# Second layer of the last four experts by column halves, first outputs by column halves, left tokens' transfer by batches

## The chip, the cores and the metric

The kernel runs on one core of a Trainium2 chip. The metric is the device time of one execution in microseconds; the time before is 535.15 us, the median of three runs (534.55 to 535.35). Engines are named as in the profile: PE is TensorE, PEld its weight load, DVE VectorE, ACT ScalarE, POOL GpSimd, SP SyncE, which issues the transfers of this kernel.

## The reference

Attention of 8 batches with 8 heads, 576 positions of 64, in which scores under the row's maximum minus tau are dropped, and on its output x (4608 tokens of 512) a soft mixture of 8 experts with 4 slots each, hidden size 1024:

```python
attn_out = _attn_ref(q, k, v, tau)                       # 8, 8, 576, 64
x = attn_out.transpose(0, 2, 1, 3).reshape(4608, 512)
logits = x @ phi                                         # 4608 x 32
d = softmax(logits, axis=0)                              # 1e-09 added to the sum
slot_input = (d.T @ x).reshape(8, 4, 512)
for e in range(8):
    h = np.maximum(slot_input[e] @ w1[e], 0.0)           # 4 x 1024
    slot_out[e] = h @ w2[e]                              # 4 x 512
c = softmax(logits, axis=1)
return c @ slot_out.reshape(32, 512)                     # 4608 x 512
```

## The kernel before

The first 470 us hold the attention and, with it, the logits and the sums of slot_input; TensorE works there nearly without a stop. The change touches nothing of it, apart from four small copies of st1 to st4 at its end. Behind it comes the tail, which is written in the order in which each engine is to run it (`manual_schedule`).

The tail works on two groups of four experts (a = 0 for experts 0 to 3, a = 1 for 4 to 7). A group's four experts stand side by side on the 128 columns of TensorE, 32 each. Both layers' weights come in units of 1 MB: four units (one for each expert, index g) for each group and half K of the contraction. A unit of w2 is a tile of 128 partitions with four rows (j) of 512 floats each; `load_unit` issues a unit's transfer on SP once the tile's former user has left it. The last four units (`LAST`: a = 1, K = 1) come in parts: j 0 and 1 of all four, 512 KB each, then j 2 and 3 of the first three; j 2 and 3 of the fourth had been loaded long before into `early`.

`stage1` is the first layer, `relu` and `hidden` bring its result onto the partitions as hz, and `stage2` the second layer. It accumulates into the PSUM tile `so`, 512 columns, over both groups, all K and j; the partitions of so hold four partial sums. The last part (a = 1, K = 1, j 2 and 3) goes into two tiles `end` (h00e and h11e), one for each half of the 512 columns, so that `so` can be copied to SBUF (`so_sb`) meanwhile. `combine` then adds end to so_sb on DVE, sums the four parts by a matmul with st4 (tile sr) and splits the result in a high and a low part `sh` for the output product (ACT writes the cast, DVE the rest).

The output product takes the 128 partitions of cT, the transposed weights c of one batch, against sh. A batch's 512 tokens are four matmuls of 128 tokens, token 4p + c for partition p, so that one partition writes four rows of out that follow each other, 8 KB. Each 128x512 result is in a tile of its own (`otile`), copied to SBUF by ACT or DVE in turn. The batches' first 512 tokens go out in transfers of 1 MB, the first two batches in smaller pieces (256, 256 and 512 KB; 512 and 512 KB). Job 8 is the left tokens, 64 of each of the eight batches. `ct()` makes the next cT: POOL a block of c two ahead, four transposes on TensorE, cast on ACT, subtraction on DVE; it stands behind the batch's output matmuls, two batches ahead, with three cT buffers.

For the left tokens 128 partitions write 8 KB each, four tokens of one batch: partition = r * 8 + b, with r from 0 to 15.

Of the kernel before, what the change touches and what calls it, by code (L numbers as in the profile page):

```python
# [838 lines left out]
def softmax_attention_soft_moe(  # L839
# [104 lines left out]
    early = wp.tile([128, 2, 512], F32, name="early")  # L944

# [4 lines left out]
    def load_unit(t):  # L950
# [554 lines left out]
    st4 = tl.tile([128, 4, 32], F32, name="st4")  # L1505
    for g in range(4):
        nc.gpsimd.tensor_copy(st4[:, g, :], st1)
# [32 lines left out]
    def ct():  # L1540
# [9 lines left out]
        t = tl.tile([128, SM], F32R, tag="cT", name=f"cT{len(cTs)}", bufs=3)  # L1550
# [54 lines left out]
    def stage2(a, K, h):  # L1605
        w = range(n_units // 2 + (a * 2 + K) * 4, n_units // 2 + (a * 2 + K) * 4 + 4)
        t = [where[i].rearrange("p (j f) -> p j f", j=4) for i in w]

        if a == NG - 1 and K == 1 and h == 1:
            for n, g in enumerate((3, 0, 1, 2)):  # L1610
                for q, dst in enumerate(end):
                    x = slice(q * DM // 2, (q + 1) * DM // 2)
                    for j in (2, 3):
                        m = (n + q) % 2 * 2 + j - 2
                        nc.tensor.matmul(
                            dst[m * 32:(m + 1) * 32, 0:DM // 2], hz[a][:, K * 4 + j, g * 32:(g + 1) * 32],
                            t[g][:, j, x] if g < 3 else early[:, j - 2, x], start=n < 2, stop=n > 1,
                            tile_position=(0, 32 * m), skip_group_check=True)
            return
        for j in (2 * h, 2 * h + 1):  # L1620
            for g in range(4):
                nc.tensor.matmul(
                    so[g * 32:(g + 1) * 32, :], hz[a][:, K * 4 + j, g * 32:(g + 1) * 32], t[g][:, j],
                    start=(a, K, j) == (0, 0, 0), stop=(a, K, j) == (NG - 1, 1, 1),
                    tile_position=(0, 32 * g), skip_group_check=True)
# [18 lines left out]
    def combine():  # L1644
# [13 lines left out]
        for n, (b, k, z) in enumerate(jobs):  # L1658
# [17 lines left out]
            if k + z == 4:  # L1676
                ct()
# [81 lines left out]
```

## Time and profile before

| | us |
|---|---|
| median of 3 runs | 535.15 |
| lowest, highest | 534.55, 535.35 |
| profiled execution, first to last instruction | 533.2 |
| difference of the median to it | 1.95 |

The page gives busy shares over the whole span: PE 97%, DVE 88%, ACT 84%, POOL 46%. They belong to the attention. For the tail one takes the windows (busy time of each engine in a stretch, the granted clock as a share of the full one, the mean busy share of the 16 DMA engines and what they moved) and the chain of waits, which goes from the last instruction back to what released it. Times are counted from the first instruction. In the names of tiles, numbers of buffers are left out: "w" is any tile of weights, "host" any of those that the outputs are gathered in.

### The profile page before, as it was taken

How to read it: one execution, taken by the hardware profiler on the slowest of the kernel's cores; microseconds unless marked ns; L12 is line 12 of the kernel's file. 1: busy time of each engine (PE TensorE's matmuls, PEld its weight loads, DVE VectorE, ACT ScalarE, POOL GpSimd, SP SyncE). 2: the span in 40 equal slices, each digit the busy share in tenths (PEclk: the TensorE clock that was granted, in tenths of full speed). 3: DMA queues.
4: the chain of work that ended last, by engine and by line, in shares of the span. 5: the costliest groups of instructions: out<-in, count | busy, mean ns of one | idle time of the engine just before them, and what ended most of it. 6: DMA issues, size and time to landing. Idle time of an engine off the chain costs nothing.

```text
span 533.2 us, 21792 instructions
## 1 busy us (share of the span) xinstructions
PE 514.7 (97%) x8877; PEld 403.5 (76%) x8877; DVE 467.3 (88%) x1311; ACT 447.4 (84%) x750; POOL 247.6 (46%) x444
## 2 busy tenths in 40 slices
PE   8999999999999999999999999999999999999881
PEld 5877888888878888888788888888788877643470
DVE  6999998999899998999899989999999999613282
ACT  3899998999899989998999989999899899612271
POOL 2475554556446454655356635554464546021030
PEclk9999999999999999999999999999999999999996
DMA  6333335333337314732953355353466315999398
GB/s 157 94 93 94 93 98 172 96 94 93 94 99 245 93 35 100 256 78 67 284 140 96 92 172 173 94 133 94 104 225 188 83 20 176 368 401 389 158 399 301
DMA packets 28868, 83.26 MB, mean 156 GB/s; under 512 B 4064, under 2 KB 12256, under 8 KB 26336
## 3 DMA queue, kind: packets, MB, share of 16 engines
q1 hardware_dynamic: 28448, 81.43, 49.5%
q8 instruction: 70, 1.15, 0.9%
q10 hardware_dynamic: 320, 0.44, 0.3%
q14 instruction: 30, 0.25, 0.2%
HBM read 72.42 MB, written 9.44 MB: 154 GB/s over the span
## 4 chain that ended last, share of the span: by engine, by line
PE 86%; DMA 4%; ACT 3%; DVE 3%; issue 2%; SPq 0%; DVEq 0%; ACTq 0%
PE ps L1068 24%; PE ps L1211 22%; PE ps L984 19%; PE ps L1234 4%; PE ps L1223 4%; PE ps L1073 3%; DMA w<-in_w 3%; PE ps L1268 2%; PE h L1579 2%; PE ps L1326 2%; PE ps L1376 2%; PE ps L1178 1%; ACT cT L1570 1%; DVE cT L1571 1%; PE ct L976 1%
## 5 line engine op out<-in xcount | busy, mean ns | idle before, releaser
L1080 DVE TENSOR_SCALAR_CACHE_REDUCE ss<-ps 128x576 f32<-128x576 f32 x288 | 208.3, 751 | 4.6 <-PE ps L1068 1.4
L1096 DVE SCALAR_TENSOR_TENSOR p<-ss,thr,p 128x576 f32<-128x576 f32 x256 | 203.6, 821 | 3.8 <-POOL thr L1093 1.6
L1093 POOL TENSOR_SCALAR thr<-nmx,pabs 128x1 f32<-128x1 f32 x288 | 136.1, 480 | 146.5 <-DVE ss L1080 143.2
L1090 ACT ACTIVATE p<-ss,nmx 128x576 f32<-128x576 f32 x256 | 188.6, 781 | 12.6 <-DVE ss L1080 11.6
L1068 PE MATMUL ps<-k,q 64*128 64x288 f32 x1024 | 154.9, 423 | 0.4
L1068 PEld LDWEIGHTS ps<-k,q 64*128 64x128 f32 x1024 | 87.5, 188 | 23.6 <-ACT pTa L989 5.1
L984 PEld LDWEIGHTS ps<-ident,p 64*128 64x128 f32 x2304 | 91.8, 138 | 17.2 <-DVE ss L1080 2.3
L984 PE MATMUL ps<-ident,p 64*128 64x64 f32 x2304 | 101.4, 223 | 0.2
L989 ACT COPY pTb<-ps 128x1024 f32<-128x1024 f32 (+1 forms) x96 | 83.8, 877 | 2.1 <-PE ps L984 0.7
L989 ACT COPY pTa<-ps 128x1024 f32<-128x1024 f32 x64 | 65.1, 1017 | 0.4 <-PE ps L984 0.2
L1211 PE MATMUL ps<-pTa,vv 128*64 128x128 f32 x992 | 61.0, 276 | 0.1
L1211 PE MATMUL ps<-pTb,vv 128*64 128x128 f32 x992 | 60.4, 274 | 0.0
L1211 PEld LDWEIGHTS ps<-pTa,vv 128*64 128x64 f32 x992 | 53.5, 137 | 5.5 <-issue 4.3
L1211 PEld LDWEIGHTS ps<-pTb,vv 128*64 128x64 f32 x992 | 53.6, 137 | 3.3 <-issue 2.8
L1263 POOL TENSOR_TENSOR x<-x,ri 128x512 f32<-128x512 f32 x31 | 37.2, 1201 | 10.3 <-ACT x L989 10.3
L1122 POOL TENSOR_SCALAR pL<-pL,ri 128x576 f32<-128x576 f32 x31 | 26.0, 840 | 15.2 <-DVE ri L1121 14.2
L1048 POOL TENSOR_SCALAR k<-k,flag 128x576 f32<-128x576 f32 x31 | 31.7, 1023 | 0.8 <-DMA k<-in_kT 0.4
L989 ACT COPY pTl<-ps 128x256 f32<-128x256 f32 x64 | 27.5, 429 | 3.3 <-PE ps L984 2.9
L1119 POOL TENSOR_SCALAR ri<-r 128x9 f32<-128x9 f32 x31 | 7.1, 229 | 45.4 <-DVE p L1096 44.6
L1223 PE MATMUL ps<-pTl,vv 64*64 64x128 f32 x496 | 26.5, 284 | 0.5 <-DVE ss L1080 0.5
L1249 ACT COPY xT<-ps 128x256 f32<-128x256 f32 x62 | 23.2, 374 | 4.4 <-PE ps L1211 2.6
L1532 POOL TENSOR_TENSOR w<-lall,crow 128x512 f32<-128x512 f32 x9 | 9.3, 1046 | 37.7 <-PE ct L976 24.4
(175 smaller groups left out, 609.0 us busy)
## 6 DMA issues: line engine op xcount, KB each, us to landing
w<-in_w SPq DMA_DIRECT2D x18, 1024.0 KB, 8.2
q<-in_qT SPq DMA_DIRECT2D x62, 288.0 KB, 4.5
vv<-in_vt SPq DMA_DIRECT2D x32, 320.0 KB, 4.8
host<-in_w SPq DMA_DIRECT2D x10, 1024.0 KB, 8.2
k<-in_kT SPq DMA_DIRECT2D x62, 144.0 KB, 4.2
out<-host SPq DMA_DIRECT2D x7, 1024.0 KB, 6.9
w<-in_w SPq DMA_DIRECT2D x7, 512.0 KB, 14.4
out<-host SPq DMA_DIRECT2D x2, 512.0 KB, 3.0
```

Of the source, the lines that this page charges most:

```text
L984: nc.tensor.transpose(out=s[:, g, c:c + 64], in_=ins[g], identity=ident[rows[g], rows[g]], tile_position=(64 * g, 0))
L989: G.add("ACT", 51 + 0.833 * n, nom, lambda: nc.scalar.copy(*io()), r, w)
L1048: sc = lambda e, kc=kc: lambda: e.tensor_scalar(out=kt.t[:, kc], in0=kt.t[:, kc], scalar1=flag8, **one)
L1068: nc.tensor.matmul(s.t[:, g, 0:HS], qt.t[rows[g], h, c * 128:(c + 1) * 128], kt.t[rows[g], h * HS:(h + 1) * HS], start=True, stop=True, ti ...
L1080: dve(678, t + OFF['mx'], [s], [ss, nmx], lambda s=s, ss=ss, nmx=nmx: nc.vector.tensor_scalar(out=ss.t.rearrange("p (a k) -> p a k", a=2), ...
L1090: G.add("ACT", 674, t + OFF['ex'], lambda sv=sv, nmx=nmx, view=view: nc.scalar.activation(view().rearrange("p (a k) -> p a k", a=2), sv(), ...
L1093: pool(250, t + OFF['th'], pre=75, fn=lambda nmx=nmx, thr=thr: nc.gpsimd.tensor_scalar(out=thr.t, in0=nmx.t, scalar1=1.0, scalar2=pabs, op ...
L1096: fn=lambda sv=sv, thr=thr, view=view, i=i: nc.vector.scalar_tensor_tensor(out=view().rearrange("p (a k) -> p a k", a=2), in0=sv(), scalar ...
L1122: pool(725, t + OFF['sc'], lambda: nc.gpsimd.tensor_scalar(out=pL.t[:, SL:SL + S], in0=pL.t[:, SL:SL + S], scalar1=ri.t[:, 8:9], **one), [ ...
L1211: nc.tensor.matmul(area(w, h, l)[rows[a]], vv.t[:, (h * 4 + kb) * 64:][:, 0:64], pT.t[:, h, kb, a * 128:(a + 1) * 128], tile_position=(0, ...
L1223: nc.tensor.matmul(area(ab[l], h, l)[rows[a]], vv.t[rows[h], SM + h * 64:][:, 0:64], pTl.t[rows[h], (l * 2 + a) * 128:][:, 0:128], tile_po ...
L1263: G.add("POOL", 1040, u + 6.8, own=f"new{j}" + group(b), r=[ri], w=[x[j]], fn=lambda: nc.gpsimd.tensor_tensor(out=wide(), in0=wide(), in1= ...
```

## The change

- The last four units of w2 come by column halves: 256 of 512 columns, all four j (512 KB in rows of 1 KB) of the first three, j 0 and 1 (256 KB) of the fourth; then the same for the other half. Eight transfers in place of seven, the same bytes.
- `so` takes the first group alone and is copied behind it. The second group goes by column halves into the two end tiles: `half(q, j)` the units of K = 0, `half_unit(q, g)` one unit of K = 1. Column half 0 is complete before half 1 begins.
- `total(q)` is combine's first part for one half; total(0) stands in the middle of half(1, .), total(1) behind the first outputs.
- `out_half(b, q)` puts out one column half of batch b, 0 to 3: two tiles of 128x2x256 with two matmuls of 256 columns each, one copied by ACT, one by DVE, and a transfer of 512 KB in rows of 1 KB. Half 0 of the four batches stands between the half_units of column half 1; half 1 behind total(1), each with a ct. Batches 4 to 7 and the left tokens go whole, by `out_whole`.
- The left tokens' transfer has b outermost, partition = b * 16 + r; cT8 is written in that order.
- st4 lies in a tile of w2 that is free there and is copied behind stage 1; otile uses so's bank in place of h11's; cT has four buffers.

The diff, cut to its core:

```diff
-        for k, h in [(i, 0)] * (i in LAST) + [(k, 1) for k in LAST[:-1]] * (i == LAST[-1]):
-            nc.sync.dma_start(where[k].rearrange("p (j f) -> p j f", j=4)[:, 2 * h:2 * h + 2],
-                              src(units[k][1])[:, 2 * h:2 * h + 2])
+        for k, q in [(i, 0)] * (i in LAST) + [(k, 1) for k in LAST] * (i == LAST[-1]):
+            js = slice(0, 2 if k == LAST[-1] else 4)
+            nc.sync.dma_start(where[k].rearrange("p (j f) -> p j f", j=4)[:, js, cols[q]], src(units[k][1])[:, js, cols[q]])
...
-        t = tl.tile([128, SM], F32R, tag="cT", name=f"cT{len(cTs)}", bufs=3)
+        t = tl.tile([128, SM], F32R, tag="cT", name=f"cT{len(cTs)}", bufs=4)
...
-            tv = t.rearrange("p (c r b) -> p b r c", c=4, b=B)
+            tv = t.rearrange("p (c b r) -> p b r c", c=4, b=B)
...
+    def product(a, K, j, g, m, w, dst, q, **kw):
+        nc.tensor.matmul(dst[m * 32:(m + 1) * 32, 0:q.stop - q.start], hz[a][:, K * 4 + j, g * 32:(g + 1) * 32], w[:, q],
+                         tile_position=(0, 32 * m), skip_group_check=True, **kw)
...
+    def half(q, j):
+        t = w2_units(NG - 1, 0)
+        for g in range(4):
+            product(NG - 1, 0, j, g, g, t[g][:, j], end[q], cols[q], start=j == 0, stop=False)
+
+    def half_unit(q, g):
+        t = w2_units(NG - 1, 1)[g]
+        for j in (2, 3, 0, 1):
+            w = early[:, j - 2] if g == 3 and j > 1 else t[:, j]
+            product(NG - 1, 1, j, g, j, w, end[q], cols[q], start=False, stop=g == 3)
+
+    def total(q):
+        x = cols[q]
+        nc.vector.tensor_tensor(out=so_sb[:, x], in0=end[q][:, 0:DM // 2], in1=so_sb[:, x], op=ALU.add)
+        w = ttile(f"sr{q}")
+        nc.tensor.matmul(w[:, 0:DM // 2], st4.rearrange("p g s -> p (g s)"), so_sb[:, x], start=True, stop=True)
+        nc.scalar.copy(sh[:, x], w[:, 0:DM // 2])
+        nc.vector.scalar_tensor_tensor(
+            out=sh[:, x], in0=sh[:, x].bitcast(F32), scalar=neg, in1=w[:, 0:DM // 2], op0=ALU.mult, op1=ALU.add)
...
+    def out_half(b, q):
+        ot = through()[b].rearrange("p (c d) -> p c d", c=4)[:, :, cols[q]]
+        for k in range(2):
+            w = otile(f"o{b}_{q}_{k}").rearrange("p (c d) -> p c d", c=2)
+            for c in range(2):
+                nc.tensor.matmul(w[:, c], cTs[b][:, token(b, 2 * k + c)], sh[:, cols[q]], start=True, stop=True,
+                                 skip_group_check=True)
+            if k:
+                nc.vector.tensor_copy(ot[:, 2 * k:2 * k + 2], w)
             else:
-                nc.sync.dma_start(out.rearrange("(b s) d -> b s d", s=S)[:, SM:S].rearrange(
-                    "b (r c) d -> r b (c d)", c=4), ot.rearrange("p c d -> p (c d)"))
+                nc.scalar.copy(ot[:, 2 * k:2 * k + 2], w)
+        nc.sync.dma_start(out[b * S:b * S + SM].rearrange("(p c) d -> p c d", c=4)[:, :, cols[q]], ot)
...
+            nc.sync.dma_start(out.rearrange("(b s) d -> b s d", s=S)[:, SM:S].rearrange(
+                "b (r c) d -> b r (c d)", c=4), ot.rearrange("p c d -> p (c d)"))
...
+    for K in range(2):
+        stage2(0, K)
+        if K == 0:
+            hidden(1)
+    nc.scalar.copy(so_sb, so)
+    for j in range(4):
+        half(0, j)
+    for g in range(4):
+        half_unit(0, g)
+    for j in range(4):
+        half(1, j)
+        if j == 1:
+            total(0)
+    for g in range(4):
+        half_unit(1, g)
+        out_half(g, 0)
+        if g < 2:
+            ct()
+    total(1)
+    for b in range(4):
+        out_half(b, 1)
+        ct()
+    for b in range(4, B + 1):
+        out_whole(b)
```

How TensorE's order moves. Before, from the last four units' second half to the second output job (h00e and h11e are the end tiles, early and w11, w5, w1 the units' tiles, w7 the hidden values, sr the sums with st4, o the outputs as job and chunk, ct a transposed block of c):

```order
L1615 MATMUL h11e_8448<-w5_114,w7_116 32x256 x2
L1615 MATMUL h00e_8447<-w1_110,w7_116 32x256 x2
L1615 MATMUL h11e_8448<-w1_110,w7_116 32x256 x2
L1651 MATMUL sr0_8548<-w3_112,st4_8278 128x256
L1651 MATMUL sr1_8552<-w3_112,st4_8278 128x256
L1664 MATMUL o0_0_0_8556<-sh_8302,cT0_8416 128x256
L1664 MATMUL o0_0_1_8559<-sh_8302,cT0_8416 128x256
L1671 MATMUL o1_0_8563<-sh_8302,cT0_8416 128x512
L1671 MATMUL o2_0_8567<-sh_8302,cT0_8416 128x512
L1671 MATMUL o2_1_8568<-sh_8302,cT0_8416 128x512
L976 MATMUL ct2_8575<-ident_61,w3_112 128x128 x4
L1671 MATMUL o3_0_8583<-sh_8302,cT1_8432 128x512
```

After, from the first unit of column half 1 to the third batch's first half:

```order
L1608 MATMUL h11e_8448<-w11_120,w7_116 32x256 x4
L1663 MATMUL o0_0_0_8563<-sh_8297,cT0_8416 128x256 x2
L1663 MATMUL o0_0_1_8567<-sh_8297,cT0_8416 128x256 x2
L977 MATMUL ct2_8574<-ident_61,w3_112 128x128 x4
L1608 MATMUL h11e_8448<-w5_114,w7_116 32x256 x4
L1663 MATMUL o1_0_0_8585<-sh_8297,cT1_8432 128x256 x2
L1663 MATMUL o1_0_1_8589<-sh_8297,cT1_8432 128x256 x2
L977 MATMUL ct3_8596<-ident_61,w3_112 128x128 x4
L1608 MATMUL h11e_8448<-w1_110,w7_116 32x256 x4
L1663 MATMUL o2_0_0_8607<-sh_8297,cT2_8573 128x256 x2
```

Before, all of the second layer lies ahead of sr and of every output. After, half_unit (h11e), four o matmuls of one batch and a ct follow each other in turn, and sr1 stands behind the fourth batch's first half:

```order
L1608 MATMUL h11e_8448<-w8_117,w7_116 32x256 x2
L1663 MATMUL o3_0_0_8620<-sh_8297,cT3_8595 128x256 x2
L1663 MATMUL o3_0_1_8624<-sh_8297,cT3_8595 128x256 x2
L1635 MATMUL sr1_8630<-w3_112 128x256
L1663 MATMUL o0_1_0_8634<-sh_8297,cT0_8416 128x256 x2
L1663 MATMUL o0_1_1_8638<-sh_8297,cT0_8416 128x256 x2
L977 MATMUL ct4_8645<-ident_61,w3_112 128x128 x4
L1663 MATMUL o1_1_0_8652<-sh_8297,cT1_8432 128x256 x2
```

From there on a batch's second half and one ct take turns.

SP's queue before, the last parts of w2 (w11 to w1) and the outputs (out; the numbers are partitions by floats):

```order
L965 DMA w11_120<-in_w2 128x1024
L965 DMA w5_114<-in_w2 128x1024
L965 DMA w1_110<-in_w2 128x1024
L1679 DMA out_0<-w10_119 128x512 x2
L1679 DMA out_0<-w10_119 128x1024
L1679 DMA out_0<-host0_7724 128x1024 x2
L1679 DMA out_0<-host1_7882 128x2048
L1679 DMA out_0<-host2_7980 128x2048
L1679 DMA out_0<-host3_8054 128x2048
L1679 DMA out_0<-host4_8062 128x2048
```

And after, from the second column half:

```order
L967 DMA w11_120<-in_w2 128x4x256
L967 DMA w5_114<-in_w2 128x4x256
L967 DMA w1_110<-in_w2 128x4x256
L967 DMA w8_117<-in_w2 128x2x256
L1669 DMA out_0<-w10_119 512x1x256
L1669 DMA out_0<-host0_7724 512x1x256
L1669 DMA out_0<-host1_7882 512x1x256
L1669 DMA out_0<-host2_7980 512x1x256
L1669 DMA out_0<-w10_119 512x1x256
L1669 DMA out_0<-host0_7724 512x1x256
```

Two whole transfers and five pieces of batches 0 to 3 have become eight halves of 512 rows of 256 floats, and the weights come as 128x4x256; the last transfer, at the end of the same queue, is 8x16x2048 for 16x8x2048.

## Rows read from the trace of the kernel before

**Rows 1.** Page, chain that ended last: share of the span by engine.

```profile
PE 86%; DMA 4%; ACT 3%; DVE 3%; issue 2%; SPq 0%; DVEq 0%; ACTq 0%
```

**Rows 2.** Chain of waits 490 to 534: start us, us, what.

```profile
481.25 15.94 DMA w<-in_w
...
501.70 0.43 DVE w L1648
...
502.18 0.71 PE sr L1651 x2
502.91 0.38 ACT sh L1652
...
503.32 0.49 DVE sh L1653
...
503.94 0.85 PE o L1664 x2
...
506.78 0.70 DVE cT L1571
...
507.62 0.64 PE ct L976 x4
```

**Rows 3.** Windows: span, length, busy of engines, granted clock, DMA share, GB/s.

```profile
40.00:100.00 60.00, 59.92 (x1144) 49.75 (x1140) 58.01 (x166) 57.09 (x98) 31.70 (x56) 1.00 0.42 111
491.40:497.20 5.80, 5.67 (x46) 1.41 (x38) 0.00 (x0) 0.00 (x0) 0.00 (x0) 1.00 1.01 408
502.00:506.00 4.00, 3.19 (x14) 2.62 (x15) 2.15 (x6) 1.94 (x5) 0.00 (x0) 1.00 0.00 0
505.00:517.00 12.00, 10.36 (x49) 8.68 (x49) 10.57 (x17) 9.01 (x18) 5.24 (x5) 1.00 0.89 356
517.00:527.00 10.00, 4.05 (x16) 2.79 (x15) 5.89 (x9) 4.49 (x8) 0.00 (x0) 0.90 1.02 416
524.00:526.00 2.00, 0.00 (x0) 0.00 (x0) 0.00 (x0) 0.00 (x0) 0.00 (x0) 0.73 1.04 434
527.00:528.00 1.00, 0.00 (x0) 0.00 (x0) 0.00 (x0) 0.00 (x0) 0.00 (x0) 0.50 1.02 262
528.00:529.00 1.00, 0.00 (x0) 0.00 (x0) 0.00 (x0) 0.00 (x0) 0.00 (x0) 0.50 1.02 197
531.00:532.00 1.00, 0.00 (x0) 0.00 (x0) 0.00 (x0) 0.00 (x0) 0.00 (x0) 0.50 0.04 16
527.00:532.00 5.00, 0.00 (x0) 0.00 (x0) 0.00 (x0) 0.00 (x0) 0.00 (x0) 0.50 0.74 208
```

**Rows 4.** Timeline of TensorE 495 to 506: start us, us, line, tile.

```profile
500.97 0.41 PE L1615 MATMUL h00e<-w,w 128*32 128x256 f32 x2 [0.53 <-DMA w<-in_w]
```

**Rows 5.** Timeline of SyncE, 66 to 90 and 495 to 534.

```profile
67.37 1.34 SPq L1425 DMA_DIRECT2D phi_sb<-in_phi  x1
69.39 0.35 SPq L1053 DMA_DIRECT2D vv<-in_vt  x1
...
505.32 1.42 SPq L1679 DMA_DIRECT2D out<-w  x3
```

**Rows 6.** DMA view 505 to 515: 40 bins of 0.25 us.

```profile
GB/s 0 0 0 0 90 385 385 377 377 401 459 393 426 393 410 99 279 442 410 377 426 393 410 393 410 393 262 524 426 328 295 524 524 426 262 328 524 426 393 360
```

**Rows 7.** Groups by form 494 to 534: line engine op names shapes, busy, mean ns.

```profile
L1671 PE MATMUL o<-sh,cT 128*128 128x512 f32 x35 | 12.3, 472 | 1.2 <-DVE cT L1571 1.2
L1675 DVE COPY host<-o 128x512 f32<-128x512 f32 x16 | 10.2, 686 | 0.2
L1671 PEld LDWEIGHTS o<-sh,cT 128*128 128x128 f32 x35 | 9.2, 301 | 2.0 <-DVE cT L1571 1.5 <-DVE host L1675 0.2
...
L1622 PE MATMUL so<-w,w 128*32 128x512 f32 x32 | 5.4, 595 | 0.2 <-DMA w<-in_w 0.2
...
L976 PEld LDWEIGHTS ct<-ident,w 128*128 128x128 f32 x28 | 3.0, 140 | 3.7 <-POOL w L1532 3.0 <-issue 0.6
L1615 PE MATMUL h00e<-w,w 128*32 128x256 f32 x12 | 2.2, 387 | 0.5 <-DMA w<-in_w 0.5
```

More of the change, by code (lines that the diff above doesn't have):

```diff
@@ L944, in softmax_attention_soft_moe @@
     early = wp.tile([128, 2, 512], F32, name="early")
+    cols = [slice(n * DM // 2, (n + 1) * DM // 2) for n in range(2)]
     def load_early():
@@ L1603, in hidden, with w2_units @@
                 )
-    def stage2(a, K, h):
+    def w2_units(a, K):
         w = range(n_units // 2 + (a * 2 + K) * 4, n_units // 2 + (a * 2 + K) * 4 + 4)
[L1607 to L1620, printed above, removed]
-            for g in range(4):
[L1622 to L1625, printed above, removed]
-        if h:
-            for i in w:
-                load_unit(where[i])
@@ new lines, in w2_units, with stage2 @@
+        return [where[i].rearrange("p (j f) -> p j f", j=4) for i in w]
+    def product(a, K, j, g, m, w, dst, q, **kw):
+        nc.tensor.matmul(dst[m * 32:(m + 1) * 32, 0:q.stop - q.start], hz[a][:, K * 4 + j, g * 32:(g + 1) * 32], w[:, q],
+                         tile_position=(0, 32 * m), skip_group_check=True, **kw)
+    def stage2(a, K):
+        t = w2_units(a, K)
+        for j in range(4):
+            for g in range(4):
+                product(a, K, j, g, g, t[g][:, j], so, slice(0, DM), start=(K, j) == (0, 0), stop=(K, j) == (1, 3))
@@ L1634, in otile @@
         k = cnt[0] % 6
-        return ps_h.tile([128, 512], F32, tag=("h01", "h10", "h11")[k // 2], name=name) if k % 2 else ttile(name)
+        return ps_h.tile([128, 512], F32, tag=("h01", "h10", "so")[k // 2], name=name) if k % 2 else ttile(name)
     def through():
@@ new lines, in out_whole @@
+    def out_whole(b):
+        ot = through()[b].rearrange("p (c d) -> p c d", c=4)
+        ws = [otile(f"o{b}_{c}") for c in range(4)]
+        for c in range(4):
+            nc.tensor.matmul(ws[c], cTs[b][:, token(b, c)], sh, start=True, stop=True)
+            if c % 2 == 0:
+                nc.scalar.copy(ot[:, c], ws[c])
+            else:
+                nc.vector.tensor_copy(ot[:, c], ws[c])
+        ct()
+        if b < B:
+            nc.sync.dma_start(out[b * S:b * S + SM].rearrange("(p c) d -> p c d", c=4), ot)
+        else:
+            nc.sync.dma_start(out.rearrange("(b s) d -> b s d", s=S)[:, SM:S].rearrange(
+                "b (r c) d -> b r (c d)", c=4), ot.rearrange("p c d -> p (c d)"))
@@ L1698, in softmax_attention_soft_moe @@
         relu(a, hp[a])
+    st4 = where[2][:, 3 * DM:3 * DM + 128].rearrange("p (g s) -> p g s", g=4)
+    for g in range(4):
+        nc.gpsimd.tensor_copy(st4[:, g, :], st1)
     ct()
@@ L1701, in softmax_attention_soft_moe @@
     end[:] = [ps_h.tile([128, 512], F32, tag=t, name=t + "e") for t in ("h00", "h11")]
-    for a in range(NG):
-        for K in range(2):
-            for h in range(2):
-                if a == NG - 1 and K == 1 and h == 1:
-                    nc.scalar.copy(so_sb, so)
-                stage2(a, K, h)
-            if a < NG - 1 and K == 0:
-                hidden(a + 1)
-    combine()
+    for K in range(2):
[7 more added lines that the diff above has]
+        half_unit(0, g)
+    for j in range(4):
+        half(1, j)
+        if j == 1:
+            total(0)
+    for g in range(4):
+        half_unit(1, g)
[5 more added lines that the diff above has]
+        out_half(b, 1)
+        ct()
+    for b in range(4, B + 1):
+        out_whole(b)
     order_all.close()
```

39 lines of the change are left out of this document (2 added, 37 removed).

## The prediction

> **What bounds the kernel now.** I read first the chain of waits of the last 44 us, then the windows of the same stretch, then single groups. Over the whole span the chain is 86% TensorE [rows 1], but the change touches nothing ahead of about 480 us, so only the tail counts. There the chain [rows 2] is to be read as four pieces. Until 497 us it is the transfer of the second layer's weights: DMA w<-in_w ends at 497.19, and the windows give 408 GB/s at a share of 1.01, so the sixteen DMA engines are full [rows 3]. From the last weights (TensorE takes the last of them at 500.97, after a wait for DMA [rows 4]) to the first output transfer runs a serial chain: add, sr, ACT sh, DVE sh, o, tile copies, first issue at 505.32 [rows 2, 5]. In it the DMA engines stand still: 502 to 506 moves nothing [rows 3]. From 506 the outputs go out. Within 505:517 356 GB/s, which is 4.27 MB: the first four batches (4 x 1.05 = 4.19 MB) are out at 516.9. Behind it, until 527, DMA is the bound (416 GB/s). Then a last piece is slow: the last transfer, of the left tokens. From 527 on 208 GB/s x 5.0 us = 1.04 MB go, which is just its 1 MB, and it ends at about 531.1; at the 434 GB/s of 524:526 the same would take 2.4 us, and it takes 4.1 [rows 3]. So two things are to be had: the 4 to 6 us in which DMA stands, and 1.7 us of the last transfer.
>
> **The change, part by part.** The profiled execution has 533.2 us between its first and last instruction, the median of the runs is 535.15; I add terms to the median and take the 1.95 us between the two as constant.
>
> *Loads by column halves.* The first half now is 1.835 MB (w8 has its other half in `early`) where 2.10 MB stood ahead of 497.19: 0.26 MB less at 408 GB/s is -0.64 us. But rows get short, 1 KB in place of 4 KB. In the transfers by row size [rows 6] four bins of 2 KB rows go at 381 GB/s on average and the next four, of longer rows, at 420: about 10% for that step, so I take 10% for 1 KB rows: 1.835 MB / 408 = 4.5 us, +0.45. First half in at 497.0, second at about 501.3 (before 500.9). Bounds: 0% to 60% (a rival, below).
>
> *The first chain.* From 497.0: four matmuls of 256 columns, half of the 0.86 us that four of 512 take (387 and 595 ns each, overlapped by two [rows 7]), then add 0.43, sr 0.71, ACT 0.38, DVE 0.49 [rows 2]. The two groups of half(1,.) that stand between the last unit and sr run during the add and cost some 0.3 beyond it. Before, this chain took 4.35 us from 500.97 to 505.32; now one add and one sr less (-0.8), half(1,.) +0.3, and a tile copy that waits for four o matmuls, not for one (+1.2): 5.1 us, so the first issue falls at 502.1, 3.2 us earlier.
>
> *The middle.* Here TensorE's order decides, since each out_half stands behind the next half_unit and ahead of a ct. A batch costs four o matmuls, whose strided weights load for 301 ns against 140 for ct [rows 7] and which follow each other at about 0.235 us, 0.94; a ct, 0.44 without its drain; a half_unit 0.43; two changes of tile shape, some 0.1 each: 2.0 us. The 512 KB that it gives go out in 1.4. Issues at 502.1, 504.1, 506.1 and, without ct, 507.4. So DMA idles again by 0.5 us three times.
>
> *The second chain.* total(1) stands behind out_half(3,0) and is serial: 0.43 + 0.71 + 0.38 + 0.49 and hand-overs, 2.3 us, and 1.95 until the first tile of the second half is out: 507.4 to 511.6. DMA idles for 2.8 us. The single serial chain has become two. Then a second half costs VectorE a tile copy of 0.69 and the subtraction of a cT of 0.70 [rows 2, 7], 1.45 us a batch, about what its transfer takes. Issues 511.6, 513.2, 514.7, 516.1; batch 4, with two tile copies on VectorE behind ct7, at 518.2, its data from 519.0. Before, it was 516.9: +2.1. A replay of the engines' queues with the same durations gives +1.3 for it; I keep 2.1. Issuing costs SP more: phi's 512 pieces took it 1.34 us where 128 took 0.35 [rows 5], about +1.0 for each of the fourteen 512-piece transfers. SP has waits of over that everywhere but in the second halves (1.34 of 1.45); +0.2 for the last of these. Bounds of the whole of this: -1.2 (the rival of the other sign) to +4.
>
> *Left tokens.* The transfer's 16x8x2048 becomes 8x16x2048, the cT8 writes keep their sizes. Lower bound 2.4 us (434 GB/s, -1.7), upper bound twice the present 4.1 (+4.1). I take the rate of its own middle, 262 and 197, mean 230 GB/s [rows 3], for all of it, since the trace has no row of eight entries and these are the nearest: 4.6 us, +0.5.
>
> *At nothing:* the st4 copies move behind the masks on GpSimd, 0.66 us ahead of blocks that TensorE needs ten us later; the otile bank and the fourth cT buffer loosen waits. If st4 were late, it would show as a wait of sr on GpSimd, worth under 0.7.
>
> Sum: 535.15 + 2.1 + 0.2 + 0.5 = 538.0 us. The gap that the change fills is given back in pieces: 3.2 us gained at the first issue, less 1.5 in the middle, 2.8 at the second chain, and the short rows and VectorE pace.
>
> **Rivals.**
>
> *The last transfer pays for eight entries.* Its rate in 527:529 at a DMA share of 1.02 means that all engines are busy and yet move half [rows 3]. If it is dealt out by the outermost index and each of eight parts goes as slowly as each of sixteen did, it takes 8.2 us: +4.1 in place of +0.5, 541.5. For it: in the tail such rates come at no other place with that share. Against it: no row shows that the outermost index deals. The Trainium skill, page "DMA: Bandwidth & Descriptors", section "Why a DMA increments its semaphore by 16 and not by 1", says that it does: the number of engines is the largest up to 16 that divides the slowest index of both sides, here eight against sixteen before. By that rule alone, with the parts at full rate, the estimate is half of 434 GB/s, 4.8 us; with the parts as slow as before, 8.2. No run here shows eight.
>
> *All transfers of 512 short rows go as the last one did.* These fourteen also have different walks on both sides, 512 rows of DRAM against 128 partitions. Nearest rows: the last transfer, 254 GB/s over its 4.1 us, and the main phase, where transfers of 64 partitions make 111 GB/s at a share of 0.42, thus 264 at a full one [rows 3]. At 254 the first half of the weights takes 2.4 us more (first issue 504.4), and a half output 2.06 us: DMA is full from 505 and is behind by 5.3 at batch 4: 535.15 + 5.3 + 0.5 = 541.0, and with the rival above 544.6. The Trainium skill, same page, section "The descriptor swizzle", says that a transfer to 128 partitions is dealt so that each engine has a port of its own, which the others need not have; the share of 1.02 at 197 GB/s agrees.
>
> *Nothing lost in transfers.* Short rows cost nothing (-0.45) and the last transfer goes at 434 GB/s (-1.7): 535.15 + 2.3 - 0.45 - 1.7 = 535.3, the same as now.
>
> *Faster: TensorE goes by columns.* Place: the middle, 502 to 511. If an o matmul of 256 columns takes half of what one of 512 does (472 ns, overlapped by two, thus 0.12 in place of 0.235) and the weights load is hidden, a batch takes 1.4 us, not 2.0, the four save 2.0 and the second halves some 1.2: batch 4's data begin at 515.8, -1.1. It decides from 0.15 us for one o: then DMA is fed without the 0.5 us gaps. With the last transfer between 2.4 and 4.6 us that is 532.4 to 534.6, middle 533.5. Against it: the weights load of 301 ns doesn't depend on columns, and TensorE loads such weights in 9.2 us for 12.3 of matmul [rows 7].
>
> **How the numbers follow.** Forecast 538.0 with 0.34; eight slow parts (541.5) 0.22; fourteen slow transfers (541.0 to 544.6) 0.14; nothing lost (535.3) 0.12; by columns (533.5) 0.18. A difference of 0.2%, 1.07 us, is about what a measurement of this kernel can tell from no change. The forecast's own range, 536.4 to 539.6, lies above it. So slower 0.34 + 0.22 + 0.14 = 0.70, same 0.12, faster 0.18. The range reaches into the last two on both sides: 532.8 to 544.6.
>
> **What will show it.** Right: first issue near 502; three short gaps and one of 2 to 3 us about 508 to 511 in the DMA windows; VectorE busy in the second halves; batch 4's transfer at about 519. Wrong: o matmuls closer than 0.15 us, so that the windows from 503 to 511 are full; loads of the last weights at under 300 GB/s; a last transfer of 2.4 us or of 8. If batch 4 starts ahead of 516.9 the forecast's sign has fallen with it, unless the last transfer takes over 5.

## The result, and the profile after

| | before | after |
|---|---|---|
| median of 4 runs, us | 534.86 | 543.06 |
| profiled execution, first to last instruction, us | 533.2 | 541.1 |
| last transfer by the windows, about, us | 4.1 | 7.4 |

The changed kernel is slower: ratio 1.0150, 95% interval 1.0136 to 1.0164, which is 8.2 us. Forecast were 2.85 us more than the 535.15 known then, 538.0; the direction was right and the size was not, though the range (to 544.6) holds the time.

Of the profile after, first the windows, to be set beside [rows 3] (columns as there):

```profile
491.00:497.00 6.00, 4.68 (x72) 2.14 (x66) 0.00 (x0) 0.59 (x1) 0.00 (x0) 1.00 1.10 350
502.00:504.00 2.00, 2.00 (x17) 1.42 (x16) 1.39 (x2) 1.03 (x3) 1.04 (x1) 1.00 0.00 0
504.00:512.00 8.00, 5.69 (x35) 4.00 (x35) 3.68 (x6) 2.56 (x6) 1.05 (x1) 0.96 0.76 262
512.00:514.00 2.00, 2.00 (x11) 2.00 (x11) 0.88 (x2) 1.27 (x3) 0.70 (x1) 0.50 0.00 0
532.00:538.00 6.00, 0.00 (x0) 0.00 (x0) 0.00 (x0) 0.00 (x0) 0.00 (x0) 0.50 0.50 157
```

The last weights, in rows of 1 KB, come at 350 GB/s where it was 408. The DMA engines still stand idle (502 to 504, and again 512 to 514), though 262 GB/s go between (504 to 512). Before, TensorE's granted clock was 1.00 in all of this stretch; now it is 0.50 in 512 to 514, which is 1.2 of 2.4 GHz. The left tokens at the end go at 157 GB/s from 532 to 538, at a DMA share of 0.50, where before the same megabyte went at 262 and 197 GB/s with a share of 1.02. This transfer begins at 531.7 and ends at about 539.1.

SP's timeline, against [rows 5] (start, length, operation, count):

```profile
502.79 0.62 SPq L1669 DMA_DIRECT2D out<-w  x1
504.93 4.41 SPq L1669 DMA_DIRECT2D out<-host  x3
513.09 0.53 SPq L1669 DMA_DIRECT2D out<-w  x1
515.29 3.75 SPq L1669 DMA_DIRECT2D out<-host  x3
520.55 5.67 SPq L1683 DMA_DIRECT2D out<-host  x4
```

The first output goes at 502.79, 2.5 us earlier than before, and batch 4 (L1683) at 520.55; its data begin at 521.3 where before they began at 516.9. Of the 7.9 us by which the span grew, some 4.75 are the later start of the last transfer (527.0 to 531.75) and some 3.2 the transfer itself.

One trace tells the first output's time only roughly. The first layer of the experts, which the change does not touch, begins at 468.85 before (first fence) and at 469.38 after (second fence):

```profile
468.85 10.51 PE L1579 MATMUL h<-w,phi_sb 128*32 128x512 f32 x96
```

```profile
469.38 10.51 PE L1577 MATMUL h<-w,phi_sb 128*32 128x512 f32 x96
```

From there to the first output it is 36.5 us before and 33.4 after. In the eight traces of this document whose order up to there is that of the kernel before (with b_batch8, b_left7, b_eight and the four b_ports) it is 35.3 to 37.0, mean 36.2; in the six with the changed order (all but a_no_half_out) 32.1 to 33.6, mean 32.9. So the first output comes 3.3 us earlier on average, and a difference of half a microsecond between two traces tells nothing here.

The chain of waits shows what lies between (columns as in [rows 2]):

```profile
481.28 15.23 DMA w<-in_w
...
498.80 0.63 PE sr L1635 x2
499.42 1.43 PE h11e L1608 x24
500.86 1.14 PE o L1663 x4
502.00 0.44 PE ct L977 x4
502.44 0.57 PE h11e L1608 x8
...
508.05 0.69 DVE host L1666
...
508.78 0.43 DVE w L1633
...
509.35 0.69 PE sr L1635 x2
...
510.05 0.38 ACT sh L1636
...
510.46 0.49 DVE sh L1637
...
511.00 1.30 PE o L1663 x4
512.30 0.85 PE ct L977 x4
```

The weights of column half 0 are there at 496.51. In the first chain, sh is ready at 500.35, but TensorE is still busy until 500.86 with the three groups of column half 1 (h11e) that stand between sr and the first o:

```profile
499.87 0.48 DVE L1637 SCALAR_TENSOR_TENSOR sh<-sh,neg,sr 128x256 fp32r<-128x256 f32 x1 [1.41 <-ACT sh L1636]
```

In the middle a batch is four o (1.14), ct (0.44) and one half_unit (0.57): 2.15 us, all TensorE. From 508.05 the second serial chain: tile copy, add, sr, ACT sh, DVE sh, and o again at 511.00. Behind it ct takes 0.85 where it took 0.44: the granted clock is 0.50 there. VectorE's timeline shows the pace of the second halves, one tile copy each:

```profile
512.34 0.69 DVE L1666 COPY w<-o 128x512 f32<-128x512 f32 x1 [1.40 <-PE o L1663]
...
514.53 0.69 DVE L1666 COPY host<-o 128x512 f32<-128x512 f32 x1
...
516.30 0.69 DVE L1666 COPY host<-o 128x512 f32<-128x512 f32 x1
...
517.75 0.69 DVE L1666 COPY host<-o 128x512 f32<-128x512 f32 x1
```

They follow each other at 2.19, 1.77 and 1.45 us, and the issues of the second halves likewise (2.20, 1.76 and 1.45).

### The profile page after: what moved, and what is told of

It reads as the page before. It is cut to its first block, busy times and chain, and to the rows that moved or that the text cites. A ratio compares the mean times of both kernels' runs of the same rounds, so it can differ in the third digit from the quotient of the medians.

```text
span 541.1 us, 21917 instructions
## 1 busy us (share of the span) xinstructions
PE 518.0 (96%) x8940; PEld 409.3 (76%) x8940; DVE 467.8 (86%) x1311; ACT 447.9 (83%) x749; POOL 247.8 (46%) x444
## 4 chain that ended last, share of the span: by engine, by line
PE 88%; DMA 3%; DVE 3%; ACT 2%; issue 1%; DVEq 0%; POOL 0%; POOLq 0%; ACTq 0%
PE ps L1069 24%; PE ps L1212 21%; PE ps L985 18%; PE ps L1235 4%; PE ps L1224 3%; PE ps L1074 3%; DMA w<-in_w 3%; PE h L1577 2%; PE ps L1269 2%; PE ps L1327 2%; PE o L1663 2%; PE ps L1377 2%; PE ps L977 1%; PE ps L1179 1%; PE h11e L1608 1%
## 5 line engine op out<-in xcount | busy, mean ns | idle before, releaser
L1049 POOL TENSOR_SCALAR k<-k,flag 128x576 f32<-128x576 f32 x31 | 32.1, 1035 | 0.2 <-DMA k<-in_kT 0.2
L1097 DVE SCALAR_TENSOR_TENSOR pL<-ss,thr,pL 128x576 f32<-128x576 f32 x32 | 26.1, 814 | 0.3
```

Of the source, the lines that this page charges most:

```text
L1049: sc = lambda e, kc=kc: lambda: e.tensor_scalar(out=kt.t[:, kc], in0=kt.t[:, kc], scalar1=flag8, **one)
L1097: fn=lambda sv=sv, thr=thr, view=view, i=i: nc.vector.scalar_tensor_tensor(out=view().rearrange("p (a k) -> p a k", a=2), in0=sv(), scalar ...
```

## Experiments

Ratios are to the kernel before on the same chip, with 95% intervals; a ratio's thousandth is 0.53 us.

### The last transfer: undone, and alone

```diff
-            tv = t.rearrange("p (c b r) -> p b r c", c=4, b=B)
+            tv = t.rearrange("p (c r b) -> p b r c", c=4, b=B)
...
-                "b (r c) d -> b r (c d)", c=4), ot.rearrange("p c d -> p (c d)"))
+                "b (r c) d -> r b (c d)", c=4), ot.rearrange("p c d -> p (c d)"))
```

> The changed kernel with one part undone: the left tokens' transfer has r outermost again (16x8x2048), cT8 written to match. Theory: of the 7.9 us that the profiled span grew, 3.3 are the last transfer itself (7.4 us from 531.7 to 539.1 where it was 4.1), because an outermost index of eight leaves half of the DMA engines without work (share 0.5). Then the last transfer takes 4.1 to 4.3 us with a share of about 1 at first, and the time is 543.1 - 3.2 = 539.8. Rival: the slow end comes with the place at the end of the queue or with the late start, not with the outermost index: 543.

In b_batch8 the same two lines are turned the other way, in the kernel before.

> The kernel before with that one part alone: 8x16x2048, cT8 to match. Theory: last transfer 7.4 us at a share of about 0.5, time 534.9 + 3.3 = 538.2. Rival (the loss comes only together with the column halves): 534.9, or with the rate that the prediction took, 4.6 us, 535.4.

Undone: 539.10, ratio 1.0091 (1.0062 to 1.0119), so 1.0150 - 1.0091 = 0.0059, 3.2 us. In the traces it is 17.2 us from batch 4's issue to the end of the span, where it is 20.55 in the changed kernel: 3.35. Alone: 538.23, ratio 1.0073 (1.0049 to 1.0096), 3.9 us. Both are as expected within their intervals. Windows of the undone form and of the one part alone, over the last transfer:

```profile
531.00:535.00 4.00, 0.00 (x0) 0.00 (x0) 0.00 (x0) 0.00 (x0) 0.00 (x0) 0.50 0.93 246
```

```profile
529.00:535.00 6.00, 0.00 (x0) 0.00 (x0) 0.00 (x0) 0.00 (x0) 0.00 (x0) 0.50 0.49 149
```

With sixteen entries the share is 0.93 and the rate 246 GB/s, with eight 0.49 and 149, in either kernel. So it is the walk that makes it slow, not the place and not the column halves. A share of one half fits eight busy engines and eight with nothing to do. The Trainium skill, page "DMA: Bandwidth & Descriptors", section "Why a DMA increments its semaphore by 16 and not by 1", states that the number of engines is the largest up to 16 that divides the slowest index of both sides; the share of 0.49 to 0.50 for eight entries agrees.

### Who sets batch 4's time: transfers or compute

```diff
-        nc.sync.dma_start(out[b * S:b * S + SM].rearrange("(p c) d -> p c d", c=4)[:, :, cols[q]], ot)
```

> The changed kernel without the eight transfers of out_half: batches 0 to 3 are computed and copied, but not written out. Theory: batch 4 is late because of the order of compute (two serial chains, TensorE's middle, VectorE's second halves), not because of the transfers with short rows. Then batch 4's transfer is still issued at 520.5 +- 0.4 and the whole is at most 0.5 us shorter (542.6). Rival: the short rows, 350 GB/s for 409, hold up the queue: batch 4 is issued over 1 us earlier, 541.5 or less.

```profile
522.00 3.04 SPq L1682 DMA_DIRECT2D out<-host  x2
```

```profile
510.79 0.67 PE L1635 MATMUL sr<-w 128*128 128x256 f32 x2 [1.31 <-DVE w L1633]
```

```profile
509.35 0.67 PE L1635 MATMUL sr<-w 128*128 128x256 f32 x2 [1.33 <-DVE w L1633]
```

This run leaves those outputs out. Expected were at most 542.6 and batch 4's issue at 520.5; in its one execution it was 543.52 and 522.00, so both were missed, but not in the direction of the rival. In this execution the tail ran later as a whole (sr1 at 510.79 for 509.35), so the measure is a distance. From the first o to sr1, which is the middle, it is 8.53 us without the transfers (from 502.26) and 8.56 with them (from 500.79). From sr1 to batch 4's issue it is 522.00 - 510.79 = 11.21 without and 520.55 - 509.35 = 11.20 with them. So in the changed kernel the order of compute sets it, and the short rows of these outputs cost nothing there.

### The second serial chain

```diff
...
-    for g in range(4):
-        half_unit(1, g)
-        out_half(g, 0)
-        if g < 2:
-            ct()
-    total(1)
+    half_unit(1, 0)
+    out_half(0, 0)
+    half_unit(1, 1)
+    out_half(1, 0)
+    ct()
+    half_unit(1, 2)
+    half_unit(1, 3)
+    added(1)
+    out_half(2, 0)
+    total(1)
+    ct()
+    out_half(3, 0)
```

(`added` is the first line of total(1), the add on DVE.)

> The changed kernel with the same work in another order: the last half_units stand together, and the second total's add and sr stand ahead of ct3 and of batch 3's first half, so that its chain runs beside them. Theory: the second serial chain with TensorE idle (508.0 to 511.0) and the granted clock of 0.5 behind it are what delays the second halves: their first issue comes at about 510.4 in place of 513.1, the clock stays at 1.00 until 520, batch 4 is issued near 517.2, time 543.1 - 3.3 = 539.8. Rival: VectorE's 1.45 us a batch or the transfers of the first halves give it back, batch 4 near 519.8 and 542.3.

539.66, ratio 1.0098 (1.0064 to 1.0132): 2.8 us won, as much as hoped within the interval, but not in the way expected. TensorE's timeline where the first halves end, with its wait in brackets, SP's issue of the first second half and of batch 4, and the windows:

```profile
508.62 2.25 PE L1668 MATMUL o<-sh,cT 128*128 128x256 f32 x8 [1.40 <-DVE cT L1569]
```

```profile
511.66 0.53 SPq L1674 DMA_DIRECT2D out<-w  x1
...
519.14 5.44 SPq L1688 DMA_DIRECT2D out<-host  x4
```

```profile
510.00:512.00 2.00, 2.00 (x11) 2.00 (x10) 1.25 (x2) 0.83 (x2) 0.13 (x1) 0.51 0.08 29
512.00:514.00 2.00, 2.00 (x11) 2.00 (x10) 1.39 (x2) 1.29 (x3) 1.17 (x2) 0.64 0.99 342
```

The first second half is issued at 511.66, not 510.4: TensorE waited 1.40 us for cT3, whose ct now stood directly ahead of its use. And the clock fell to 0.51 all the same. Batch 4 is issued 16.8 us behind the first output (502.38), where the changed kernel took 17.8, so this trace shows 1.0 of the 2.8 us; where the rest comes from is not shown. So a second form, with ct3 ahead of the last half_unit (the diff is to the first form):

```diff
     half_unit(1, 0)
     out_half(0, 0)
+    ct()
     half_unit(1, 1)
     out_half(1, 0)
+    half_unit(1, 2)
     ct()
-    half_unit(1, 2)
     half_unit(1, 3)
     added(1)
     out_half(2, 0)
     total(1)
-    ct()
     out_half(3, 0)
```

> As the run before with the second total early, but ct3 stands ahead of the last half_unit and not behind sr, since there TensorE waited 1.4 us for cT3 and the granted clock still fell to 0.5. Theory: with no idle TensorE between the first and the second halves the clock stays at 1.00, the second halves follow each other at 1.45 us from the first on, and batch 4 is issued 3 us earlier than in the changed kernel: 543.1 - 3.2 = 539.9, or 1 us below the run with ct3 late. Rival: VectorE is the bound there and gives it back: the same as that run.

538.09, ratio 1.0058 (1.0042 to 1.0075): 4.9 us below the changed kernel by the ratios.

```profile
510.00:512.00 2.00, 2.00 (x15) 1.98 (x14) 1.31 (x2) 1.51 (x3) 1.04 (x1) 1.00 0.92 314
512.00:514.00 2.00, 2.00 (x12) 1.99 (x12) 1.91 (x4) 1.54 (x3) 1.36 (x2) 1.00 0.99 339
```

```profile
503.02 0.62 SPq L1674 DMA_DIRECT2D out<-w  x1
...
511.08 0.53 SPq L1674 DMA_DIRECT2D out<-w  x1
...
517.81 5.43 SPq L1688 DMA_DIRECT2D out<-host  x4
```

The clock is 1.00 throughout, and batch 4 is issued 14.8 us behind the first output (517.81 - 503.02) where the changed kernel took 17.8 (520.55 - 502.79): 3.0 us of the 4.9 are seen in this trace (its execution was the slowest of four). The time expected was 539.9. The second halves do not follow each other at 1.45 us from the first on, as expected: the first takes 1.79 here too (511.08 to 512.87). And with the chain gone the DMA engines are all but full (0.92 and 0.99, at 314 and 339 GB/s).

### The clock by itself

```diff
+    def warm(n):
+        w = ps_h.tile([128, 512], F32, tag="h00", name="warm")
+        for i in range(n):
+            nc.tensor.matmul(w, cTs[2][:, 0:128], cTs[2], start=True, stop=True)
...
+        if q:
+            warm(4)
         w = ttile(f"sr{q}")
...
+        if q:
+            warm(3)
```

> The changed kernel with seven matmuls more, whose results nobody reads, four ahead of sr1 and three behind it, where TensorE stood idle for 1.3 and 1.0 us. Theory: the clock that fell to 0.50 in 512 to 514 made the first two second halves 2.2 and 1.76 us long where the third took 1.45; with the clock held they take 1.5 each, and the time falls by 0.8 to 1.0, less some 0.2 for the matmuls: 542.3. Rival: VectorE and the hand-overs set these times, the clock is a bystander: 543.1 to 543.5.

```profile
512.00:514.00 2.00, 2.00 (x14) 1.98 (x14) 1.74 (x3) 1.70 (x4) 1.58 (x2) 1.00 0.44 155
```

```profile
501.70 0.62 SPq L1678 DMA_DIRECT2D out<-w  x1
...
511.90 0.53 SPq L1678 DMA_DIRECT2D out<-w  x1
513.68 3.43 SPq L1678 DMA_DIRECT2D out<-host  x3
518.62 5.42 SPq L1692 DMA_DIRECT2D out<-host  x4
```

540.89, ratio 1.0111 (1.0095 to 1.0126), 2.1 us below the changed kernel. With the seven idle matmuls the clock stays at 1.00, and the issues of the second halves begin at 511.90 and 513.68, 1.78 us apart where it was 2.20 and 1.5 were expected. From the first second half to batch 4 it takes 6.72 us (511.90 to 518.62) where the changed kernel takes 7.46 (513.09 to 520.55), and the run with sixteen entries, whose order is the same up to there, 7.62. So the clock costs 0.7 to 0.9 us, near the 0.8 to 1.0 expected, and it is no bystander. The time fell by more than that: in this execution the weights and with them the first output came 1.1 us earlier (501.70 for 502.79), which is within what traces of one order show.

### Both causes undone

The two diffs above together (the left tokens' walk and the second form of the order).

> The changed kernel with both causes undone: the second total early with ct3 ahead of the last half_unit, and the left tokens' transfer with r outermost again. Theory: the two account for all of the loss, 4.9 us (1.0150 to 1.0058) and 3.2 (1.0150 to 1.0091), and column halves by themselves gain and lose nothing: 543.1 - 8.1 = 535.0, a ratio of 0.999 to 1.002. Rival: the short rows of 7.3 MB (350 for 409 GB/s, some 3 us) still have to be paid: 537.5 or more.

536.93, ratio 1.0039 (1.0021 to 1.0057): 2.1 us stay, and neither expectation was met. The single runs would have summed to 0.0092 + 0.0059, and together they are worth 0.0111. The medians of the spans, from the first instruction to the last, differ by less: 534.65 against 533.0, 1.65 us; the other half microsecond lies outside the span. The profiled execution was the slowest of ten. In it the first layer of the experts begins late:

```profile
471.71 10.51 PE L1577 MATMUL h<-w,phi_sb 128*32 128x512 f32 x96
```

From there to the end of the span it is 537.1 - 471.7 = 65.4 us, in the changed kernel 541.1 - 469.4 = 71.7, and before (first layer from 468.85) 64.35. In the tail alone 1.0 us is left, in this one execution; its runs spread from 535.4 to 538.9, and why the attention ended later in this one was not looked into. In this order the transfers are the bound where they were not in the changed kernel:

```profile
512.00:520.00 8.00, 7.85 (x42) 7.25 (x41) 6.83 (x10) 6.42 (x12) 3.14 (x3) 1.00 0.98 333
```

The four second halves are 2.1 MB. At 333 GB/s that is 6.3 us and at 408 it would be 5.1: an estimate of 1.1 us that the short rows of these outputs cost here. No run has both causes undone and these rows whole, so this is not shown.

### The price of short rows

```diff
-            nc.sync.dma_start(where[k].rearrange("p (j f) -> p j f", j=4)[:, 2 * h:2 * h + 2],
-                              src(units[k][1])[:, 2 * h:2 * h + 2])
+            for x in (slice(0, 256), slice(256, 512)):
+                nc.sync.dma_start(where[k].rearrange("p (j f) -> p j f", j=4)[:, 2 * h:2 * h + 2, x],
+                                  src(units[k][1])[:, 2 * h:2 * h + 2, x])
```

> The kernel before; only the seven transfers of the last w2 units are each cut into two by columns, 128x2x256, rows of 1 KB in place of 4 KB. Theory: the size of the rows alone brings the rate from 409 to 350 GB/s, whether the walks of both sides agree (as here, 128 and 128) or not (512 rows in the changed kernel): the last weights land 1.5 us later for 3.67 MB, 534.9 + 1.5 = 536.4. Rival: it is the 512 rows against 128 partitions: the rate stays at 400 or more and the time at 534.9.

```diff
-                nc.sync.dma_start(out[b * S:b * S + SM].rearrange("(p c) d -> p c d", c=4)[:, k:k + z], ot)
+                for x in cols if b < 4 else [slice(0, DM)]:
+                    nc.sync.dma_start(out[b * S:b * S + SM].rearrange("(p c) d -> p c d", c=4)[:, k:k + z, x], ot[:, :, x])
```

> The kernel before, only the output transfers of batches 0 to 3 are each cut into column halves, rows of 1 KB as in the changed kernel (4.19 MB). Theory: where the DMA engines are the bound, rows of 1 KB cost 4.19 MB / 350 - 4.19 MB / 409 = 1.7 us: 536.5. With the loads (0.7 us measured) that is the part of the loss that stays when the second chain and the last transfer are undone (1.0039, 2.1 us). Rival: for writes the rows' size costs nothing, 534.8, and what stays is the idle time of the DMA engines between the halves.

```profile
491.00:497.00 6.00, 6.00 (x59) 1.84 (x54) 0.16 (x1) 0.00 (x0) 0.00 (x0) 1.00 1.06 350
```

```profile
508.00:512.00 4.00, 3.46 (x17) 2.78 (x16) 3.71 (x7) 2.87 (x7) 1.92 (x2) 1.00 1.01 340
```

The loads alone: 535.46, ratio 1.0017 (1.0003 to 1.0030), 0.9 us for 1.5 expected, at the same 350 GB/s with 128 rows on both sides as the changed kernel has with 512 against 128. The rate is as expected; the 0.9 us are not seen in its trace, where the first output comes 36.1 us behind the first layer's start, in the middle of the 35.3 to 37.0 of the runs without the cut. The outputs alone, where DMA is the bound: 536.83, ratio 1.0043 (1.0030 to 1.0057), 2.3 us for 1.7 expected, at 340 GB/s. So it is the size of the rows, not the walk: the rate falls from 408 by a seventh for the reads and by a sixth for the writes.

### Why the left tokens' transfer is slow before the change too

This no longer concerns the change, but the 1.6 us that both kernels leave. Six forms of the kernel before were run.

```diff
-    blocks = [(slice(row(b), row(b) + 4), 4) for b in range(B)] + [(slice(N9 - 1, NR, N9), B // 2)]
+    blocks = [(slice(row(b), row(b) + 4), 4) for b in range(B)]
+    blocks.insert(7, (slice(N9 - 1, NR, N9), B // 2))
...
```

> The kernel before with the left tokens as the last but one: their transfer stands ahead of batch 7's, its walk unchanged (16x8x2048). Theory: what is slow in it is that its sixteen parts get into each other's way while nothing else is in flight; with a transfer of 1 MB queued behind, engines that are through early go on with that, and up to 1.6 of its 4.1 us are won: 533.3. Rival: it takes its 4.1 us wherever it stands, 534.9.

```profile
523.50:527.60 4.10, 0.00 (x0) 0.00 (x0) 0.00 (x0) 0.00 (x0) 0.00 (x0) 0.70 1.01 260
```

535.20, ratio 1.0010 (0.9997 to 1.0024). The transfer takes its 4.1 us at a share of 1.01 and 260 GB/s in the middle of the queue too; the whole transfer behind it does not fill in, as the rival has it: at this share the engines are busy all the time.

```diff
-                nc.sync.dma_start(out.rearrange("(b s) d -> b s d", s=S)[:, SM:S].rearrange(
-                    "b (r c) d -> r b (c d)", c=4), ot.rearrange("p c d -> p (c d)"))
+                for x in range(B):
+                    nc.sync.dma_start(out[x * S + SM:(x + 1) * S].rearrange("(r c) d -> r (c d)", c=4),
+                                      ot.rearrange("p c d -> p (c d)")[x::B])
```

> Control for the run with 16 ports: the kernel before, only the left tokens' transfer is cut into eight of 128 KB, one for each batch, on the partitions as they were (r * 8 + b, step eight), so that each of sixteen parts meets the same partner at a port as before. Theory of the ports: 4.1 us as before, 534.8. Rival, that one batch at a time is better for DRAM: 533.3 here too.

```diff
...
+                    b = h * 4 + x
+                    nc.sync.dma_start(out[b * S + SM:(b + 1) * S].rearrange("(r c) d -> r (c d)", c=4),
+                                      ot.rearrange("p c d -> p (c d)")[32 + x:96:4])
...
```

> The kernel before, with the left tokens laid on partitions 32 to 95 of two tiles, token chunk r of batch b on partition 32 + 4r + b mod 4, and written by eight transfers of 128 KB, one for each batch, 16 partitions with a step of four each (the output matmuls take eight windows of 128 columns, of which 64 count, where before there were four). Theory: the last transfer is slow before the change too because pairs of its sixteen parts meet at one port of the SBUF (partitions 32 apart); here the sixteen parts of each transfer are on sixteen different ports, so the last 1 MB goes at over 400 GB/s, 2.5 us for 4.1: 534.8 - 1.5 = 533.3. Rival: it is the walk through DRAM or the late small pieces that are slow: 534.8 or, for the added copies and issues, more.

```profile
528.00:532.00 4.00, 0.00 (x0) 0.00 (x0) 0.00 (x0) 0.00 (x0) 0.00 (x0) 0.50 0.89 232
```

```profile
528.00:531.00 3.00, 0.00 (x0) 0.00 (x0) 0.00 (x0) 0.00 (x0) 0.00 (x0) 0.50 0.60 243
```

b_eight 535.05, ratio 1.0009 (0.9994 to 1.0025); b_ports 534.76, 1.0002 (0.9988 to 1.0016). The windows tell more than the times: with partitions eight apart (b_eight, first fence) 232 GB/s at a share of 0.89, by division 261 for full engines; with partitions 32 to 95 in steps of four (b_ports, second fence) 243 at 0.60, thus 405, about the rate of a whole transfer. Both write the same places of DRAM in the same pieces, so it is the partitions that decide; but the engines of b_ports are idle for part of the time. The Trainium skill, page "SBUF — State Buffer", section "Door 1: The DMA port swizzle", states that partitions 32 apart share a port, and that 64 apart are on another; both rates agree with it. To feed the engines, two more forms: the left tokens as seventh of nine outputs (b_ports6), and the last four of the eight transfers issued by ScalarE (b_ports_two).

> The kernel before with the left tokens on sixteen ports by eight transfers, as in the run before, now as the seventh of nine outputs, ahead of batches 6 and 7. There the eight transfers went out one each 0.6 us, as SP could issue them, at a DMA share of 0.58, and so the 1.6 us were not won. Theory: in the queue's middle SP is some 4 us ahead of the transfers, so the issues are hidden, the left tokens take 2.5 us, the last transfer is a whole batch at 410 to 434 GB/s: 534.8 - 1.6 = 533.2, ratio 0.997. Rival: the issues (8 x 0.6 = 4.8 us) or the four copies more on each of VectorE and ScalarE hold up batch 6: 534.8 or more.

> The kernel before with the left tokens last, on sixteen ports by eight transfers, but four of them issued by SP and four by ScalarE, which is through with its copies by then. Theory: both earlier forms were held by SP's 0.6 us an issue (the DMA share was 0.5 to 0.6, the rate for a busy engine that of whole transfers); with two engines issuing, 128 KB come each 0.3 us, as fast as they can be moved, and the last 1 MB takes 2.5 to 2.9 us where it took 4.1: 534.6 - 1.3 = 533.3, ratio 0.9975. Rival: the issues of the two engines take turns, or the transfers meet each other at the ports after all: 534.6 or more.

b_ports6: 535.95, ratio 1.0025 (1.0015 to 1.0036), slower; SP issues one each 0.6 us and holds up the batches behind. b_ports_two: 535.38, ratio 1.0016 (1.0004 to 1.0027). A window of it, and SP's wait:

```profile
528.00:529.00 1.00, 0.00 (x0) 0.00 (x0) 0.00 (x0) 0.00 (x0) 0.00 (x0) 1.00 0.99 410
```

```profile
SPq L1679 <- DMA out<-host: 2.9, 1, 2.9
```

Until 529 it goes at 410 GB/s; but SP, with two of its four issued, waits 2.9 us, from 527.1 to 530.0, for an earlier transfer to land before it issues the third, and the engines run dry. A last form has four of the eight ahead of batch 7's transfer:

> The kernel before with the left tokens on sixteen ports, the first four of their eight transfers ahead of batch 7's and the last four behind it, these issued by SP and ScalarE in turn. In the run before six of eight went at 410 to 434 GB/s and then SP waited 2.9 us for an earlier transfer to land before it could issue the seventh; here the transfers eight places ahead of the last ones have landed long before. Theory: DMA is full to the end and the last 1 MB costs 2.5 to 2.8 us for 4.1: 534.6 - 1.4 = 533.2, ratio 0.9975. Rival: another wait of the issuing engines takes its place, 534.6.

534.32, ratio 1.0004 (0.9993 to 1.0015). In its trace the second half goes at 393 to 418 GB/s to the end, but the first four, at 0.6 us an issue, leave the engines at a share of 0.65 in 524 to 526. None of the forms beats the kernel before.

## Why the prediction was right and wrong

**Right.** That the idle stretch would be given back, and where: a second serial chain of 4.28 us from the fourth first half's issue (508.81) to the first second half's (513.09), where 4.2 were forecast, and batch 4 later than before. That in the middle TensorE's order decides and not the transfers: the run without them has the same distances. The rival that eight parts pay was priced at 8.2 us and came to 7.4.

**Right by luck: the first output.** It was forecast 33.25 us behind the first layer's start of the kernel before (502.1), and it is 33.4 here. But the weights of column half 0 came 1.0 us earlier than forecast, counted from the first layer (27.1 for 28.15), although their rate fell by a seventh and not by the tenth taken from [rows 6]; and the chain behind them took 6.3 us for 5.1. Two half_units stand behind the last weights where the forecast had one, so the add begins 1.5 us behind them; and the three groups behind sr hold TensorE for half a microsecond after sh is ready.

**Wrong: the left tokens (+0.5, measured +3.2).** The step is "I take the rate of its own middle, 262 and 197, mean 230 GB/s [rows 3], for all of it". The row had been made by sixteen parts; with eight it went at 157. Whether the outermost index deals the parts to the engines was open in the rows; the value chosen was nearest to no change, and the rival, with 0.22, was the case. With it the sum would have been 541.5.

**Wrong: batch 4's data (+2.1, measured +4.4).** 0.5 of the 4.4 is that the tail began later in this execution (469.38 for 468.85), by no more than the traces of the kernel before and its forms differ (468.9 to 470.3). The rest is 1.8 more than forecast, in two places. The second halves and batch 4 behind them took 7.46 us for 6.6: TensorE's idle time in the second chain was followed by a clock of 0.50, which no step had, and with the idle matmuls it is 6.72. The middle took 6.0 us for 5.3. In it the "0.235 us" at which o matmuls follow each other held for three of four; but the first stands 0.34 ahead of the second (starts at 500.79, 501.13, 501.37 and 501.60), and a batch took 2.15 us for 2.0. And the last batch, without ct, took 1.7 where "507.4" puts 1.3; by the forecast's own terms it is 2.0 - 0.44, nearly 1.6.

**Left out.** Behind batch 4 the DMA share is 0.94 to 0.99 until 526, where it was 1.02, and the last transfer starts another 0.35 us later. The issues of 512 rows took SP 0.53 to 0.62 us where 128 rows take 0.33 to 0.35, not the 1.34 of phi's load, so the +0.2 was for nothing.

**The rivals that fell.** Transfers of 512 rows against 128 partitions as slow as the last one: 350 GB/s with either walk. TensorE by columns: an o matmul of 256 columns is followed by the next after 0.235 us, just as one of 512 (before: 506.24, 506.47, 506.71), and its weights load takes 0.31 to 0.33 us in both kernels. Nothing lost in transfers: both kinds are slower.

**Open.** The two causes undone together win 5.9 us by the ratios (6.3 in the tail of the profiled executions), where singly they win 8.1 (7.9). What takes the other 2 us was not settled. The outputs' short rows, once DMA is the bound, can be some 1.1 us of it by the estimate above; the first output comes up to 1.7 us earlier or later in traces of one order, so a remainder of this size cannot be read from single traces. The loads' short rows are not shown to be a part.

## What to carry to other kernels

Cutting a product by columns to start its output early doubles what is serial behind it: here a second chain of adds and casts, and twice as many output matmuls, each followed by the next as late as one of full width, took back all of the gain. Before a transfer's walk is turned, look at how many entries its outermost index has on both sides: with eight the trace shows a DMA share of one half. A rate in a row belongs to the walk that made it; for another walk it is a bound, not a value.

## What the runs showed of the hardware

- Rows of 1 KB go at 350 GB/s (reads, with either walk) and 340 (writes) with all engines busy, against 408 for rows of 4 KB (reads, before, 491.4 to 497.2) and 416 for rows of 8 KB (writes, before, 517 to 527).
- A transfer of 1 MB with an outermost index of eight: share 0.49 to 0.50, 149 to 157 GB/s; of sixteen: share 0.93 to 1.02, 246 to 260.
- Transfers of sixteen partitions in steps of four from 32 on: 405 GB/s by division for full engines; in steps of eight: 261.
- Issuing an output took SP 0.33 to 0.35 us for 128 rows, 0.53 to 0.62 for 512 rows of 1 KB, and mostly 0.5 to 0.6 for 16 rows of 8 KB, so that eight such transfers in place of one leave the engines at a share of 0.60 (b_ports).
- After TensorE had waited 1.33 us for the add and 0.98 us for sh, its granted clock fell from 1.00 (2.4 GHz) to 0.50 (1.2 GHz); with seven idle matmuls at these two places it stayed at 1.00, and 0.7 to 0.9 us were won.
- Output matmuls with weights in strides of four follow each other at 0.235 us with 256 columns and with 512: no gain from fewer columns.
